# Pairing heads for larger weight loads, and untying slot copies from the next load, in a linear-attention and expert kernel

## The chip, the cores and the metric

The kernel runs on one core of one Trainium2 chip. The metric is the device time of one execution in microseconds (us); lower is better. A core has five engines with a queue each: TensorE (PE; weight loads are listed as PEld), VectorE (DVE), ScalarE (ACT), GpSimd (POOL) and SyncE (SP), and 16 DMA engines that all queues share. An engine works through its own instructions in the order in which the program gives them, and waits on semaphores for the others.

## The reference

Eight sequences, each of 576 positions, 8 heads of 64. Attention without a score matrix, then one expert of eight for each whole sequence:

```python
q_s = softmax(q, over head_dim);  k_s = softmax(k, over seq)
kv  = einsum('bhsd,bhse->bhde', k_s, v)
x   = einsum('bhsd,bhde->bhse', q_s, kv)        # -> [B, S, D = 512]
logits = x.mean(axis=1) @ w_gate                # [B, 8]
e_idx  = argmax(logits)                         # one expert for each sequence
out[b] = gate_w[b] * relu(x[b] @ w1[e]) @ w2[e] # w1 512x1024, w2 1024x512
```

The inputs are float32 and fixed; on them the eight sequences choose the experts 2 3 3 1 3 3 4 6. So 0, 1, 3, 6 and 7 need an expert whose weights were not there before, and 2, 4 and 5 use expert 3 again.

## The kernel before, in words

A sequence `b` is handled as two halves, `n = 2b` and `n = 2b + 1`, of four heads each; a half has four 64-row groups, kept as two "pairs" of heads side by side on 128 partitions.

- `load(n)` fetches q, k and v of a half on SyncE's queue: three transfers of 128 partitions x 1152 floats. Three buffers of each exist.
- `exp_q`, `exp_k` (ScalarE), `cast_v` (GpSimd) and `scale_q` (a sum and a reciprocal on VectorE, a multiply on GpSimd) prepare a half. `kvt_step` makes kv and transposes q on TensorE ("a kv step" here), with `kv_out` and `t_out` on VectorE. `x_step(n, g)` makes one quarter of x in the one `x` bank of PSUM, which VectorE empties with a running sum for the mean.
- `gate_step(b)` is the gate: four small matmuls, a chain of tiny VectorE operations for the argmax and for the look in `hist`, the history of which expert each of the five weight slots holds. GpSimd then reads the expert into a register and issues the loads of w1 (L314) and w2 (L325) into slot `b % 5`; when the expert is already in some slot, the loads are skipped at run time but still issued. These transfers convert float32 to float16 on the way. `gate_exp`, `gate_split` and `gate_spread` make the softmax weight.
- `fetch` (L367) copies w1 or w2, in two parts each, from the slot found at run time to the sequence's own slot; a sequence with fresh weights copies its slot onto itself. Since the source is a run-time index, the framework lets the copy wait for every weight load issued ahead of it.
- `moe(b)` is the expert: eight groups of `x @ w1` (L381, L386; Relu on ScalarE L390), then four outputs of `h @ w2` (L400, scaled on ScalarE L407) and a tail (L415, L420). Outputs leave on SyncE's queue.

The order of the work is written by hand. `moe(b)` yields 17 times (8 groups, twice in each of 4 outputs, once after the tail), so "unit" 17 b + m is the place after yield m of sequence b, and `at(t, f)` puts a piece of the attention of later sequences at a unit. All five engines keep the order in which these pieces are written. Pieces at the same unit keep the order of the `at` calls: those of the loop over sequences come ahead of the fetches.

Of the kernel before, what the change touches and what calls it, by code (L numbers as in the profile page):

```python
# [10 lines left out]
FP16 = mybir.dt.float16  # L11
# [8 lines left out]
def kernel(  # L20
# [15 lines left out]
    nc = tc.nc  # L36
# [8 lines left out]
    ND = D // 128  # L45
    NS = 5
    IN_RANGE = "max_index over a row of 8 gives 0 to 7, and the columns past the slots never hold the maximum"

    consts = ctx.enter_context(tc.tile_pool(name="consts", bufs=1))
# [29 lines left out]
    nc.vector.memset(ones_row, 1.0)  # L79
    hist = consts.tile([1, 8], FP32)  # L80
    nc.vector.memset(hist, -1.0)
    own = consts.tile([1, NS, 8], FP32)
    nc.vector.memset(own, 0.0)
    for n in range(NS):
# [9 lines left out]
    w1_all = consts.tile([128, NS, ND, F], FP16, name="w1_all")  # L94
    w2_all = consts.tile([128, NS, NF, D], FP16, name="w2_all")

    wg_sb = consts.tile([128, ND, E], FP32)
    wg_src = moe_w_gate.rearrange("(i h g e) n -> i h e g n", i=2, h=2, g=2)

    def load_wg():  # L100
        for i in range(2):
            for h in range(2):
                nc.scalar.dma_start(
                    out=wg_sb[64 * h:64 * h + 64, 2 * i:2 * i + 2, :], in_=wg_src[i, h]
                )

    def pair_src(t, b, i):

        return t[b].rearrange("(i n g) (p j) d -> i (g p) n (j d)", i=2, n=2, p=64)[i]

    out_p = out.rearrange("b (p j) d -> b p j d", j=J)

    ins, halves, seqs = {}, {}, {}

    def load(n, names="qkv"):
        if n >= 2 * B:
            return
        b, i = divmod(n, 2)
        for name in names:
            x = in_pool.tile([128, 2, J * Dh], FP32, name=f"{name}_in")  # L120
            nc.sync.dma_start(out=x, in_=pair_src({"q": q, "k": k, "v": v}[name], b, i))
            ins[n, name] = x.rearrange("p n (j d) -> p n j d", j=J)
# [140 lines left out]
    def gate_step(b):  # L263
        pooled = seqs[b]["pooled"] if b else seqs["pooled"]
        pg = bank("x") if b else seqs["qb"][0][:, 32:64]
        for c in range(ND):
            nc.tensor.matmul(
                pg[0:1, 0:E], lhsT=pooled[:, c:c + 1], rhs=wg_sb[:, c, :],
                start=(c == 0), stop=(c == ND - 1),
            )  # L270
        zz = gat_pool.tile([1, E], FP32, name="zz")
        nc.vector.tensor_single_scalar(out=zz, in_=pg[0:1, 0:E], scalar=1.0 / S, op=ALU.mult)
        mx8 = gat_pool.tile([1, 8], FP32, name="mx8")
        nc.vector.max(out=mx8, in_=zz)
        eidx = gat_pool.tile([1, 8], U32, name="eidx")
        nc.vector.max_index(out=eidx, in_max=mx8, in_values=zz)
        slot = b % NS
        sidx = None
        if b:
            same = gat_pool.tile([1, 8], FP32, name="same")  # L280
            nc.vector.tensor_tensor(
                out=same, in0=hist, in1=eidx[0:1, 0:1].to_broadcast([1, 8]), op=ALU.is_equal
            )
            score = gat_pool.tile([1, 8], FP32, name="score")
            nc.vector.scalar_tensor_tensor(
                out=score, in0=same, scalar=2.0, in1=own[:, slot], op0=ALU.mult, op1=ALU.max
            )
            top = gat_pool.tile([1, 8], FP32, name="top")
            nc.vector.max(out=top, in_=score)
            fresh = gat_pool.tile([1, 1], U32, name="fresh")  # L290
            nc.vector.tensor_single_scalar(out=fresh, in_=top[:, 0:1], scalar=1.0, op=ALU.is_equal)
            sidx = gat_pool.tile([1, 8], U32, name="sidx")
            nc.vector.max_index(out=sidx, in_max=top, in_values=score)
        nc.vector.tensor_copy(out=hist[:, slot:slot + 1], in_=eidx[0:1, 0:1])
        nmx = gat_pool.tile([1, 1], FP32, name="nmx")
        nc.vector.tensor_single_scalar(out=nmx, in_=mx8[:, 0:1], scalar=-1.0, op=ALU.mult)
        e_val = nc.values_load(
            eidx[0:1, 0:1], engines=[ET.Pool], min_val=0, max_val=E - 1,
            skip_runtime_bounds_check_because=IN_RANGE,
        )  # L300
        kw = {}
        if b:
            f_val = nc.values_load(  # L303
                fresh, engines=[ET.Pool], min_val=0, max_val=1,
                skip_runtime_bounds_check_because="is_equal gives 0 or 1",
            )
            kw = dict(cond=(f_val == 1))
        w1_src = moe_w1[ds(e_val, 1)].rearrange("o (i h g e) f -> i h e (o g) f", i=2, h=2, g=2)
        nh = 1 if b else 2
        for fh in range(nh):  # L310
            fs = slice(fh * F // nh, (fh + 1) * F // nh)
            for i in range(2):
                for h in range(2):
                    nc.gpsimd.dma_start(  # L314
                        out=w1_all[64 * h:64 * h + 64, slot, 2 * i:2 * i + 2, fs], in_=w1_src[i, h][:, :, fs], **kw
                    )
        seqs[b].update(zz=zz, nmx=nmx, sidx=sidx, e_val=e_val, kw=kw)
        if b:
            load_w2(b)

    def load_w2(b):
        w2_src = moe_w2[ds(seqs[b]["e_val"], 1)].rearrange("o (c p) n -> p (o c) n", p=128)
        for hf in range(2):
            cs = slice(4 * hf, 4 * hf + 4)
            nc.gpsimd.dma_start(out=w2_all[:, b % NS, cs], in_=w2_src[:, cs], **seqs[b]["kw"])  # L325

    def warm(count):

        pw = bank("ht")
        for n in range(count):  # L330
            nc.tensor.matmul(pw[:, 0:128], lhsT=ident, rhs=blkmask, start=True, stop=True)

    def gate_exp(b):
        ex = gat_pool.tile([1, E], FP32, name="ex")
# [23 lines left out]
    def fetch(b, w_all, part):  # L358

        if "src" not in seqs[b]:  # L360
            seqs[b]["src"] = nc.values_load(
                seqs[b]["sidx"][0:1, 0:1], engines=[ET.DVE], min_val=0, max_val=NS - 1,
                skip_runtime_bounds_check_because=IN_RANGE,
            )
        half = w_all.shape[2] // 2
        cs = slice(part * half, (part + 1) * half)
        nc.vector.tensor_copy(  # L367
            out=w_all[:, b % NS, cs],
            in_=w_all[:, ds(seqs[b]["src"], 1), cs].rearrange("p o c f -> p (o c) f"),
        )  # L370

    def moe(b):
        xt = seqs[b]["xt"]
# [57 lines left out]
    NU = 17  # L431
    ticks = {}

    def at(t, fn, *args):
        ticks.setdefault(t, []).append((fn, args))

    def at_gate(t, b):
        at(t, gate_step, b)
        at(t + 1, gate_exp, b)
        at(t + 2, gate_split, b)  # L440
        at(t + 4, gate_spread, b)
# [3 lines left out]
    at(3.5, gate_spread, 0)  # L445
    at_gate(2, 1)
    for b in range(2, B):
        u = 24 if b == 2 else 34 + 15 * (b - 3)
        for i in range(2):
            n, t = 2 * b + i, u + 4 * i  # L450
            at(t, kvt_step, n)
            for g in range(2):
                at(t + 2 + g, x_step, n, g)
            at(t - 4.2, exp_q, n)
            at(t - 4.2, cast_v, n)
            at(t - 3.2, exp_k, n)
            if n + 3 < 2 * B:
                at(t - 3.2, load, n + 3)
            at(t - 2.8, scale_q, n, nc.gpsimd)
        at_gate(u + 8, b)  # L460
    for b in range(1, B):
        for part in range(2):
            at(NU * b - 2 + part, fetch, b, w1_all, part)
            at(NU * b + 0.5 + part, fetch, b, w2_all, part)
    times = sorted(ticks)
    done = [0]

# [13 lines left out]
    with tc.manual_schedule(engines={ET.PE, ET.DVE, ET.Activation, ET.Pool, ET.SP}):  # L481

        warm(55)
        exp_q(0)
        scale_q(0, nc.vector)
        exp_k(0)
        exp_q(1)
        cast_v(0)
        scale_q(1, nc.gpsimd)
        load(3)  # L490
        t_step(0)
        q_sum_step(0)
        kv_step(0)
        exp_k(1)
        cast_v(1, True)
        x_step(0, 0)
        t_step(1)
        q_sum_step(1)
        kv_step(1)
        x_step(0, 1)  # L500
        pool_step()
        cast_v(2)
        gate_step(0)
        exp_q(2)
        x_step(1, 0)
        exp_k(2)
        x_step(1, 1)
        scale_q(2, nc.vector)
        exp_q(3)
        kv_step(2)  # L510
        exp_k(3)
        scale_q(3, nc.vector)
        cast_v(3, True)
        t_step(2)
        gate_exp(0)
        kv_step(3)
        x_step(2, 0)
        gate_split(0)
        t_step(3)
        x_step(2, 1)  # L520
        load_w2(0)
        for b in range(B):
            for m, _ in enumerate(moe(b)):
                run_ticks(NU * b + m + 1)
            if b == 0:
                for n in (4, 5, 6):
                    load(n)


# [28 lines left out]
```

## Time and profile before

| | |
|---|---|
| time, median of 3 runs | 256.33 us (255.81 to 257.01) |
| profiled execution, its time | 256.26 us |
| its span, first to last instruction | 254.6 us |
| TensorE busy, mean granted clock | 184.9 us, 0.868 |
| VectorE, ScalarE, GpSimd busy | 112.3, 113.7, 68.1 us |
| moved by DMA | 48.55 MB in 28790 packets |

In the profile's lines, `out<-in` are tiles by the program's names, `xN` is a count, and in a timeline the first two numbers are the start and the length in us; brackets hold the idle time of the engine before the line and what ended it. A line of waits reads: engine and line, what it waited for, us in total, times, longest. The granted clock is 1.00 at full speed. `w_all` stands for both weight tiles.

### The profile page before, as it was taken

The numbers are of one execution on the slowest core, as the hardware profiler recorded it, in microseconds if no ns is written. First come the engines' busy times: TensorE is split into PE (matmuls) and PEld (weight loads), VectorE is DVE, ScalarE is ACT, GpSimd is POOL, SyncE is SP. The second block draws the span as 40 slices with busy tenths as digits, with TensorE's granted clock in tenths as the row PEclk, the third lists the DMA queues.
The fourth block names the chain that finished last, engine by engine and source line by source line (L and its number), as shares of the span: only waits on it lengthen the run. The fifth ranks groups of instructions, "written<-read, shape, count | busy, mean of one in ns | idle before, by whom it ended". The sixth has DMA issues, their size and how long they took to land. (4 is left out here: it accounts for less than half of the span.)

```text
span 254.6 us, 4684 instructions
## 1 busy us (share of the span) xinstructions
PE 184.9 (73%) x1703; PEld 98.3 (39%) x1703; DVE 112.3 (44%) x357; ACT 113.7 (45%) x177; POOL 68.1 (27%) x88
## 2 busy tenths in 40 slices
PE   7465899939863699467398499869958820499991
PEld 7342454514431354224144254434534410145541
DVE  1759450223784765170644955576526600610000
ACT  3759654529343337513057127722842410034641
POOL 1327314005623122921006300630573060000000
PEclk9755699997996899989689979997999985589998
DMA  6997989999999912999607940850499389006134
GB/s 220 390 391 176 143 135 177 242 372 392 391 393 300 344 46 50 203 290 296 236 0 205 370 170 3 261 182 24 67 169 214 71 126 197 7 0 160 28 82 103
DMA packets 28790, 48.55 MB, mean 191 GB/s; under 512 B 3168, under 2 KB 10336, under 8 KB 28768
## 3 DMA queue, kind: packets, MB, share of 16 engines
q1 hardware_dynamic: 19456, 37.76, 44.0%
q0 software_dynamic: 8736, 10.49, 25.6%
q8 instruction: 13, 0.21, 0.3%
q10 hardware_dynamic: 576, 0.02, 0.1%
q14 instruction: 9, 0.07, 0.1%
HBM read 61.88 MB, written 9.44 MB: 280 GB/s over the span
## 5 line engine op out<-in xcount | busy, mean ns | idle before, releaser
L381 PE MATMUL mm<-xt,w_all 128*128 128x512 f16 x256 | 75.6, 426 | 17.7 <-DVE w_all L367 13.1
L390 ACT ACTIVATE hsb<-mm 128x512 f16<-128x512 f32 x64 | 37.8, 597 | 75.5 <-PE mm L381 75.3
L400 PE MATMUL mm<-w_all,hsb 128*128 128x512 f16 x256 | 59.4, 379 | 0.0
L381 PEld LDWEIGHTS <-w_all 128*128 128x128 f16 x256 | 22.2, 106 | 58.2 <-issue 28.5
L367 DVE COPY w_all<-w_all 128x2048 f16 x28 | 20.8, 748 | 41.3 <-DMA w_all<-in_moe_w_dram 25.1
L407 ACT ACTIVATE osb<-mm,gate 128x512 f32<-128x512 f32 x32 | 22.0, 686 | 33.8 <-PE mm L400 27.6
L314 POOL DMA_DIRECT2D w_all<-in_moe_w_dram x36 | 15.2, 427 | 76.2 <-DMA w_all<-in_moe_w_dram 34.1
L147 POOL TENSOR_TENSOR eq<-eq,qsi 128x1152 f16<-128x1152 f16 x13 | 27.8, 2139 | 27.1 <-DVE qsi L146 21.9
L400 PEld LDWEIGHTS <-hsb 128*128 128x128 f16 x256 | 23.2, 98 | 25.8
L134 POOL CAST va<-v_in 128x1152 f16<-128x1152 f32 x14 | 16.7, 1192 | 32.4 <-DMA v_in<-in_v_dram 32.2
L386 PEld LDWEIGHTS <-w_all 128*128 128x128 f16 x256 | 17.7, 105 | 18.2 <-issue 5.6
L232 DVE CUSTOM_DVE_ANT_0 xt<-x,ones_f 128x576 f16<-128x576 f32 x26 | 19.4, 744 | 12.2 <-PE x L222 12.2
L221 PE MATMUL x<-qt,kv 128*128 128x512 f16 x32 | 14.8, 462 | 13.7 <-DVE qt L191 5.5
L144 DVE TENSOR_REDUCE qs<-eq 128x18 f32<-128x1152 f16 x16 | 21.5, 1345 | 6.4 <-ACT eq L126 6.4
L126 ACT ACTIVATE eq<-q_in 128x1152 f16<-128x1152 f32 x16 | 18.6, 1160 | 6.2 <-DMA q_in<-in_q_dram 6.2
L386 PE MATMUL ht<-xt,w_all 128*128 128x64 f16 x256 | 19.2, 201 | 0.0
L138 ACT ACTIVATE ek<-k_in 128x1152 f16<-128x1152 f32 x16 | 18.6, 1162 | 0.8 <-DMA k_in<-in_k_dram 0.8
L170 DVE RECIPROCAL icv<-kv 128x1 f32<-128x1 f32 x30 | 4.9, 162 | 30.3 <-PE kv L183 29.0
L162 PE MATMUL kv<-va,ek 64*128 64x129 f16 x270 | 13.1, 248 | 6.3 <-POOL va L134 4.4
L162 PEld LDWEIGHTS <-ek 64*128 64x128 f16 x288 | 11.3, 110 | 11.3 <-issue 9.1
L183 PE MATMUL kv<-ident,eq 64*128 64x64 f16 x270 | 7.8, 203 | 8.5 <-POOL eq L147 5.2
L352 PE MATMUL x<-hl,ones_row 1*128 1x2 f16 x8 | 1.4, 171 | 14.7 <-DVE hl L344 14.7
(79 smaller groups left out, 146.7 us busy)
## 6 DMA issues: line engine op xcount, KB each, us to landing
q_in<-in_q_dram SPq DMA_DIRECT2D x16, 576.0 KB, 7.7
k_in<-in_k_dram SPq DMA_DIRECT2D x16, 576.0 KB, 8.4
v_in<-in_v_dram SPq DMA_DIRECT2D x16, 576.0 KB, 8.8
w_all<-in_moe_w_dram POOLq DMA_DIRECT2D x16, 512.0 KB
out_dram<-osb SPq DMA_DIRECT2D x64, 128.0 KB, 5.7
w_all<-in_moe_w_dram POOLq DMA_DIRECT2D x28, 256.0 KB
w_all<-in_moe_w_dram POOLq DMA_DIRECT2D x8, 128.0 KB
out_dram<-osb_t SPq DMA_DIRECT2D x16, 64.0 KB, 4.1
```

What stands on the lines that cost most here:

```text
L126: nc.scalar.activation(out=eq.rearrange("p j n d -> p n j d"), in_=ins.pop((n, "q")), func=AF.Exp)
L138: nc.scalar.activation(out=ek.rearrange("p j n d -> p n j d"), in_=ins.pop((n, "k")), func=AF.Exp)
L144: nc.vector.tensor_reduce(out=qs, in_=eq, op=ALU.add, axis=AX.X)
L147: eng.tensor_tensor(out=eq, in0=eq, in1=qsi.unsqueeze(3).to_broadcast([128, J, 2, Dh]), op=ALU.mult,)
L162: nc.tensor.matmul(kps[g][:, 0:129], lhsT=ek[r, j], rhs=va[r, j], start=(j == 0), stop=(j == J - 1),)
L232: nc.vector.tensor_tensor_reduce(out=xt[:, c, :], in0=px[:, 0:S], in1=ones_f32.to_broadcast([128, S]), scale=1.0, scalar=0.0, op0=ALU.mult ...
L367: nc.vector.tensor_copy(out=w_all[:, b % NS, cs], in_=w_all[:, ds(seqs[b]["src"], 1), cs].rearrange("p o c f -> p (o c) f"),)
L381: nc.tensor.matmul(phm, lhsT=w1_sb[:, c, fsl], rhs=xt[:, c, 0:SM], start=(c == 0), stop=(c == ND - 1),)
L386: nc.tensor.matmul(pht[:, fc * ST:(fc + 1) * ST], lhsT=w1_sb[:, c, fsl], rhs=xt[:, c, SM:S], start=(fc == 0 and c == 0), stop=(fc == NF - ...
L390: nc.scalar.activation(out=hsb[:, fc, 0:SM], in_=phm, func=AF.Relu)
L400: nc.tensor.matmul(po, lhsT=hsb[:, fc, st * 128:st * 128 + 128], rhs=w2_sb[:, fc, :], start=(fc == 0), stop=(fc == NF - 1),)
L407: nc.scalar.mul(osb, po, gate)
```

## The change

1. The heads of a half are paired otherwise: half `i` now holds heads 2i, 2i+1 and 4+2i, 4+2i+1, in place of 4i to 4i+3. A 64-row half of the partitions then needs one block of w1's rows, and w1 comes in 2 DMAs for 4 (4 for 8 in sequence 0); with the 2 of w2 a sequence's weights are 4 DMAs. The gate's weights come in 2 for 4.
2. At gate `b` the entry of slot `(b + 2) % 5` is taken out of the history, and a slot copy of `b` is declared independent of the loads of `b + 1` that were issued ahead of it. With the draw above the same sequences load and skip.
3. Half 4 (the first of sequence 2) is loaded ahead of sequence 0's expert, but SyncE first waits for a tiny copy out of w1 of sequence 0. Halves 5 and 6 follow at unit 14, in place of all three after sequence 0.
4. The units move. Sequence 2's kv steps stand at 20 and 28 (24 and 28 before), sequence 3's at 33 and 38 (34 and 38), later ones 14 units apart and 5 within a sequence (15 and 4); x steps follow by 2 and 4 units (2 and 3). Preparation comes 1.2 units earlier, the multiply of `scale_q` 1.4. The gates of 2 to 7 stand at 33, 43, 57, 71, 85, 99 (32, 42, 57, 72, 87, 102). Fetches of w1 stand at 17 b - 0.8 and - 0.6 (17 b - 2 and - 1), of w2 at 17 b + 1 and + 2 (+ 0.5 and + 1.5).

```diff
+    held = consts.tile([1, 8], FP16)
...
-    wg_src = moe_w_gate.rearrange("(i h g e) n -> i h e g n", i=2, h=2, g=2)
+    wg_src = moe_w_gate.rearrange("(h c e) n -> h e c n", h=2, c=ND)
...
-        return t[b].rearrange("(i n g) (p j) d -> i (g p) n (j d)", i=2, n=2, p=64)[i]
+        return t[b].rearrange("(n i g) (p j) d -> i (g p) n (j d)", i=2, n=2, p=64)[i]
...
         nc.vector.tensor_copy(out=hist[:, slot:slot + 1], in_=eidx[0:1, 0:1])
+        gone = (b + 2) % NS
+        nc.vector.memset(hist[:, gone:gone + 1], -1.0)
...
-            for i in range(2):
-                for h in range(2):
-                    nc.gpsimd.dma_start(
-                        out=w1_all[64 * h:64 * h + 64, slot, 2 * i:2 * i + 2, fs], in_=w1_src[i, h][:, :, fs], **kw
-                    )
+            for h in range(2):
+                issued[b].append(nc.gpsimd.dma_start(
+                    out=w1_all[64 * h:64 * h + 64, slot, :, fs], in_=w1_src[h][:, :, fs], **kw
+                ))
...
+    def hold_loads():
+        nc.sync.dma_start(out=held, in_=w1_all[64:65, 0, ND - 1, 0:8])
...
-        nc.vector.tensor_copy(
+        copy = nc.vector.tensor_copy(
             out=w_all[:, b % NS, cs],
             in_=w_all[:, ds(seqs[b]["src"], 1), cs].rearrange("p o c f -> p (o c) f"),
         )
+        for load_inst in issued.get(b + 1, ()):
+            tc.declare_no_dep(copy.ins, load_inst.ins, reason="...")
...
-        u = 24 if b == 2 else 34 + 15 * (b - 3)
+        u = 20 if b == 2 else 33 + 14 * (b - 3)
         for i in range(2):
-            n, t = 2 * b + i, u + 4 * i
+            n, t = 2 * b + i, u + i * (8 if b == 2 else 5)
             at(t, kvt_step, n)
             for g in range(2):
-                at(t + 2 + g, x_step, n, g)
-            at(t - 4.2, exp_q, n)
-            at(t - 4.2, cast_v, n)
-            at(t - 3.2, exp_k, n)
+                at(t + 2 + 2 * g, x_step, n, g)
+            at(t - 5.4, exp_q, n)
+            at(t - 5.4, cast_v, n)
+            at(t - 4.4, exp_k, n)
             if n + 3 < 2 * B:
-                at(t - 3.2, load, n + 3)
-            at(t - 2.8, scale_q, n, nc.gpsimd)
-        at_gate(u + 8, b)
+                at(t - 4.4, load, n + 3)
+            at(t - 4.2, scale_q, n, nc.gpsimd)
+        at_gate(t + 5, b)
     for b in range(1, B):
         for part in range(2):
-            at(NU * b - 2 + part, fetch, b, w1_all, part)
-            at(NU * b + 0.5 + part, fetch, b, w2_all, part)
+            at(NU * b - 0.8 + 0.2 * part, fetch, b, w1_all, part)
+            at(NU * b + 1 + part, fetch, b, w2_all, part)
+    at(14, load, 5)
+    at(14, load, 6)
...
         load_w2(0)
+        hold_loads()
+        load(4)
         for b in range(B):
             for m, _ in enumerate(moe(b)):
                 run_ticks(NU * b + m + 1)
-            if b == 0:
-                for n in (4, 5, 6):
-                    load(n)
```

More of the change, by code (lines that the diff above doesn't have):

```diff
@@ L97 @@
     wg_sb = consts.tile([128, ND, E], FP32)
-    wg_src = moe_w_gate.rearrange("(i h g e) n -> i h e g n", i=2, h=2, g=2)
+    wg_src = moe_w_gate.rearrange("(h c e) n -> h e c n", h=2, c=ND)
     def load_wg():
-        for i in range(2):
-            for h in range(2):
-                nc.scalar.dma_start(
-                    out=wg_sb[64 * h:64 * h + 64, 2 * i:2 * i + 2, :], in_=wg_src[i, h]
-                )
+        for h in range(2):
+            nc.scalar.dma_start(out=wg_sb[64 * h:64 * h + 64], in_=wg_src[h])
     def pair_src(t, b, i):
-        return t[b].rearrange("(i n g) (p j) d -> i (g p) n (j d)", i=2, n=2, p=64)[i]
+        return t[b].rearrange("(n i g) (p j) d -> i (g p) n (j d)", i=2, n=2, p=64)[i]
     out_p = out.rearrange("b (p j) d -> b p j d", j=J)
-    ins, halves, seqs = {}, {}, {}
+    ins, halves, seqs, issued = {}, {}, {}, {}
     def load(n, names="qkv"):
@@ L307, in gate_step @@
             kw = dict(cond=(f_val == 1))
-        w1_src = moe_w1[ds(e_val, 1)].rearrange("o (i h g e) f -> i h e (o g) f", i=2, h=2, g=2)
+        w1_src = moe_w1[ds(e_val, 1)].rearrange("o (h c e) f -> h e (o c) f", h=2, c=ND)
         nh = 1 if b else 2
+        issued[b] = []
         for fh in range(nh):
             fs = slice(fh * F // nh, (fh + 1) * F // nh)
-            for i in range(2):
-                for h in range(2):
-                    nc.gpsimd.dma_start(
-                        out=w1_all[64 * h:64 * h + 64, slot, 2 * i:2 * i + 2, fs], in_=w1_src[i, h][:, :, fs], **kw
-                    )
+            for h in range(2):
+                issued[b].append(nc.gpsimd.dma_start(
+                    out=w1_all[64 * h:64 * h + 64, slot, :, fs], in_=w1_src[h][:, :, fs], **kw
+                ))
         seqs[b].update(zz=zz, nmx=nmx, sidx=sidx, e_val=e_val, kw=kw)
@@ L324, in load_w2 @@
             cs = slice(4 * hf, 4 * hf + 4)
-            nc.gpsimd.dma_start(out=w2_all[:, b % NS, cs], in_=w2_src[:, cs], **seqs[b]["kw"])
+            issued[b].append(
+                nc.gpsimd.dma_start(out=w2_all[:, b % NS, cs], in_=w2_src[:, cs], **seqs[b]["kw"])
+            )
     def warm(count):
@@ L370, in fetch @@
         )
+        for load_inst in issued.get(b + 1, ()):
+            tc.declare_no_dep(
+                copy.ins, load_inst.ins,
+                reason="the slot that b + 1 loads into is taken out of the history before b looks for its source",
+            )
     def moe(b):
```

## The prediction, made before the change was timed

> **What bounds the kernel now.** I read the page's busy shares and DMA queues, then the chain that ended last, the waits, the TensorE timeline, and last the busy time between the moments at which each sequence's expert matmuls begin (found in that timeline).
>
> ```profile
> span 254.6 us, 4684 instructions
> PE 184.9 (73%) x1703; PEld 98.3 (39%) x1703; DVE 112.3 (44%) x357; ACT 113.7 (45%) x177; POOL 68.1 (27%) x88
> q1 hardware_dynamic: 19456, 37.76, 44.0%
> q0 software_dynamic: 8736, 10.49, 25.6%
> ```
>
> TensorE is busy 73%, and the two large queues fill the 16 DMA engines for 69.6% of the span, 177 us. No engine is full, so it is waits that count. The chain's middle, then the waits that matter:
>
> ```profile
> 206.59 8.23 DMA w_all<-in_moe_w_dram
> 214.82 3.12 issue
> 217.94 0.70 DVE w_all L367
> ...
> 219.64 0.21 DVE hl L344
> ...
> 219.89 0.16 PE x L352
> ```
>
> ```profile
> PE x L352 <- DVE hl L344: 14.7, 1, 14.7
> PE mm L381 <- DVE w_all L367: 13.1, 6, 6.1
> PE x L221 <- DVE qt L191: 5.5, 1, 5.5
> PE mm L381 <- ACT hsb L390: 4.2, 1, 4.2
> PE x L221 <- DVE pooled L232: 4.5, 5, 1.1
> ```
>
> In the chain the slot copy of sequence 6 (L367) starts only when sequence 7's weights have landed; behind it in VectorE's queue stands sequence 7's gate split (L344), for which TensorE waits 14.7 us in the middle of sequence 6. Six other waits, 13.1 us, are the first matmul of a sequence waiting for its copies. 5.5 us is TensorE waiting for VectorE while that waits for sequence 3's w2; 4.2 us is ScalarE's exp of sequence 2 standing ahead of a Relu until its q has landed. The last row is the x bank: up to 1.1 us when two quarters of x follow too closely.
>
> Stages: start of sequence 0's matmuls to 1's, and so on, the last to the end.
>
> ```profile
> 29.44:47.15 17.71, 17.71 (x129) 8.95 (x127) 5.35 (x25) 9.88 (x19) 3.90 (x6) 0.97 1.01 172
> 47.15:80.33 33.18, 21.55 (x202) 10.89 (x200) 15.93 (x42) 16.39 (x24) 10.02 (x11) 0.92 1.06 363
> 80.33:111.06 30.73, 23.17 (x238) 12.52 (x239) 16.53 (x57) 13.87 (x21) 12.26 (x12) 0.92 0.68 182
> 111.06:145.05 33.99, 24.43 (x206) 11.97 (x206) 17.67 (x50) 12.62 (x20) 8.84 (x11) 0.85 0.73 222
> 145.05:172.33 27.28, 22.58 (x237) 12.05 (x237) 16.33 (x54) 12.68 (x20) 6.77 (x10) 0.94 0.50 164
> 172.33:198.79 26.46, 22.35 (x206) 11.22 (x206) 14.86 (x48) 12.53 (x20) 10.41 (x10) 0.94 0.60 115
> 198.79:233.34 34.55, 19.07 (x122) 9.02 (x122) 7.47 (x26) 8.36 (x16) 3.95 (x6) 0.75 0.51 92
> 233.34:254.57 21.23, 15.91 (x114) 7.90 (x112) 0.00 (x0) 8.97 (x15) 0.00 (x0) 0.95 0.34 80
> ```
>
> The first two columns are length and TensorE's busy time, the last three granted clock, DMA share, GB/s. A bare sequence is 15.9 us of matmuls. Busy time holds slow matmuls too:
>
> ```profile
> 116.56 0.70 PE L162 MATMUL kv<-va,ek 64*128 64x129 f16 x18
> 117.46 1.04 PE L381 MATMUL mm<-xt,w_all 128*128 128x512 f16 x4
> ...
> 204.00 1.03 PE L381 MATMUL mm<-xt,w_all 128*128 128x512 f16 x4
> 219.98 1.89 PE L381 MATMUL mm<-xt,w_all 128*128 128x512 f16 x4
> ```
>
> Four matmuls take 1.03 us, and 1.89 after the long wait. Some two groups run so after each wait of about 1.7 us or more: I charge 1.7 us. A kv step costs 117.46 - 116.56 = 0.9.
>
> **The change, part by part.** Units are the yields, 17 per sequence.
>
> *Slot copies freed.* Gate 7 stands at 99 now, ahead of both fetches of 6 (101.2 to 104); gate 6 at 85, ahead of the w2 fetch of 5 (86, 87). With the ordering gone these copies need only their own load. Load 6 has a whole stage to land and load 7 more, so the 14.7 us go, and 1.7 of slow matmuls behind them. The history costs one more tiny memset per gate, in VectorE idle time.
>
> *Four weight DMAs for six.* Same bytes, same 4 KB rows, issued from GpSimd. Its value lies at gates on the path:
>
> ```profile
> 72.89 0.34 PE L267 MATMUL x<-wg_sb,pooled 128*1 128x8 f32 x8
> 78.08 0.05 POOL L314 DMA_DIRECT2D w_all<-in_moe_w_dram  x1 [1.39 <-DMA w_all<-in_moe_w_dram]
> 79.58 1.42 DVE L367 COPY w_all<-w_all 128x2048 f16 x2 [2.07 <-DMA w_all<-in_moe_w_dram]
> 96.88 0.27 PE L267 MATMUL x<-wg_sb,pooled 128*1 128x8 f32 x5
> 99.77 2.77 POOL L314 DMA_DIRECT2D w_all<-in_moe_w_dram  x4 [9.22 <-DVE hl L343]
> 102.73 1.52 POOL L325 DMA_DIRECT2D w_all<-in_moe_w_dram  x2 [0.18 <-DVE qs L144]
> 110.31 1.42 DVE L367 COPY w_all<-w_all 128x2048 f16 x2 [0.56 <-DMA w_all<-in_moe_w_dram]
> 122.21 0.69 DVE L367 COPY w_all<-w_all 128x2048 f16 x1 [8.23 <-DMA w_all<-in_moe_w_dram]
> 200.78 0.34 PE L267 MATMUL x<-wg_sb,pooled 128*1 128x8 f32 x8
> ```
>
> Skipped loads (gate 2) cost 1.5 us from the first of four issues to the copy; two cost 0.75. Issued w1 pieces take 2.77/4 = 0.69 each with 128 rows; one of twice the rows costs between 0.69 and 1.38, and I take 0.75, because a w2 piece of 512 rows takes 1.52/2 = 0.76. So each gate gains 0.75 us skipped and 1.2 issued; where the gate is off the path this is worth nothing, as matmuls cover it. At the start, two gate-weight DMAs fewer on ScalarE's queue: between 0 and 1.3 us, I take 0, since inputs are still arriving.
>
> *Third sequence's loads early.* Sequence 2's first half (1152 floats on 128 partitions, three times: 1.77 MB) is issued once w1 of sequence 0 lands, before 29.44, where it was issued behind sequence 0's outputs. At the 363 GB/s of stage 1 it takes 4.9 us of DMA time from the weights of 0 and 1; some is free:
>
> ```profile
> 36.00:38.00 2.00, 2.00 (x21) 1.05 (x18) 0.49 (x3) 1.20 (x2) 1.20 (x2) 1.00 0.14 21
> 44.53 0.69 ACT L407 ACTIVATE osb<-mm,gate 128x512 f32<-128x512 f32 x1 [1.04 <-PE mm L400]
> L126 ACT ACTIVATE eq<-q_in 128x1152 f16<-128x1152 f32 x16 | 18.6, 1160 | 6.2 <-DMA q_in<-in_q_dram 6.2
> L144 DVE TENSOR_REDUCE qs<-eq 128x18 f32<-128x1152 f16 x16 | 21.5, 1345 | 6.4 <-ACT eq L126 6.4
> 142.69 2.30 DVE L367 COPY w_all<-w_all 128x2048 f16 x1
> ```
>
> SyncE holds nothing else while it waits; the outputs come later. But the exp of half 4 now stands in stage 0 (14.6), and its q sums (15.8) just ahead of the fetch of sequence 1. ScalarE is free of its third output at 45.2; exp to 46.4, reduce to 47.7, reciprocal 48.0; two copies at the chain's 0.70 end at 49.4. That delays sequence 1 from 47.15 to 49.5. Its weights were there at 47.15; pushed back by 4.9 less the 1.7 left free at 36 to 38 they come by 50.4 at worst. The 4.2 us in stage 1 go.
>
> A GpSimd multiply beside a copy stretches it: 2.30 us at 142.69 against 0.70. The Trainium skill, "SBUF — State Buffer", section "Who interferes with whom", says that a copy in a two-port mode and GpSimd take one pair of ports in turns for whole instructions; the trace agrees (2.30). By that rule, freed copies that fall beside GpSimd's descriptor writing would pay 1.6 each, and the sum would be some 5 us longer.
>
> **The stages anew** (full-speed work, then waits).
> - 0: 17.7 + 2.4 (above) = 20.1.
> - 1: work 21.0 (21.55 less 1.7 slow, one kv step and quarter steps more); slow 1.7; behind w2 of 1, which the loads of half 5 now meet, between 0 and their 4.9, I take 1.5, as VectorE needs it only after six groups; 0.5 for the x bank. Gate 2 now ends the stage. Its load could be issued 99.77 - 96.88 = 2.9 after the gate's matmul, as at gate 3; with 0.75 for the skipped pieces and a copy 4.4, against 79.58 - 72.89 + 0.7 = 7.4 before. A kv step (0.9) and the gate itself (0.3) fill part: wait 3.2. 27.9.
> - 2: gate 3 to copies was 110.31 - 96.88 = 13.4; less 1.2 issue, plus a copy, 12.9. Up to the gate 11.7 of work (9.6 of the bare sequence, a kv step 0.9, x steps and gate 1.2), 1.7 slow, 0.8 bank. 27.1.
> - 3: work 20.9 (24.43 less two slow phases), slow 1.7. w2 of 3 was copied 25.3 after its gate (122.21 - 96.88). One of the two input loads that shared that window now comes ahead of the gate; between 20.4 (4.9 less) and 25.3 I take 22.5. That is 22.5 - 12.9 = 9.6 into the stage; with a copy and an x step VectorE is free at 11.1, and TensorE needs it at 8.8 (slow 1.7, six groups, a kv step): wait 2.3, slow 1, bank 1, copies of 4 behind a kv step 1.5. 28.4.
> - 4: 22.58 less 1.7 slow and one kv step: 20.0; slow 1.7, bank 0.8, copies behind an x step 1.5. 24.0.
> - 5: 22.35 less slow and an x step: 20.5; slow 1.7, bank 0.8; GpSimd now casts half 14 before it issues load 6. 23.0.
> - 6: bare 15.9, gate pieces and an x step 0.3, copies 0.3. 16.5.
> - 7 and end: 21.2.
>
> Sum 188.2; with 29.4 ahead, span 217.6. The profiled execution lies 1.7 above its span (256.26 against 254.6, the median at 256.33): 219.3, say **219**.
>
> **The rivals.**
> *A. The ordering stays, in fact.* The copies of 5 and 6 then wait for loads 6 and 7, since both gates come first now. Gate 7 to copy was 217.94 - 200.78 = 17.2 us. Sequence 5 loses that less 4 us of matmuls, plus 1.7; sequence 6's start the 13.4 of a w1 less 2.8. 219 + 15 + 11 = 245. For it: the copy reads a slot picked at run time, so every load could be its source. Against: load 7's slot is named out of bounds by the diff.
> *B. The early stages keep their waits.* If w2 of 3 still takes 25.3 and sequence 2 starts at 80.33 as now (3.2 later), plus 3 for slow matmuls: 219 + 2.8 + 3.2 + 3 = 228. For it: DMA share 1.01 and 1.06 in stages 0 and 1.
> *C. Freed copies collide with descriptor writing:* four by 1.6, 225 at most.
> *D. Slower: the new w1 pieces move at less than half speed,* if a 1 MB piece of 64 partitions spreads worse. w1 took 110.31 - 99.77 = 10.5. A factor f adds 10.5(f-1) at the starts of 1 and 3, and the same less 8.6 and 6.6 of slack at 6 and 7 (gates 1.0 and 19.5 into stage 5, 13.4 to the copies, stages of 23.0 and 16.5): at f = 2.25 these make 13.1 + 13.1 + 4.5 + 6.5 = 37, no gain; at 2.5, 16 + 16 + 7 + 9 = 48, 267. Against: pieces of 64 partitions and 4 KB rows are what is moved already. The Trainium skill, "DMA: Bandwidth & Descriptors", section "Rules for kernel authors", says that halves of the partitions share the same 16 engines either way; by that rule the factor is 1. No trace here shows the new piece.
>
> **How the numbers follow.** Forecast 0.68 (209 to 226 alone), C 0.10, B 0.13, A 0.05, D 0.03, otherwise no change 0.01. The low end, 207: stage 0's 2.4, the 1.5 in each of 1, 3 and 4, and 2.3 with two slow phases all absent (12). The high end takes in B with a lock or two: 233. The runs shown spread by 0.47%, so under 0.5% tells nothing. Faster 0.96, within 0.01, slower 0.03.
>
> **What would show it.** TensorE's wait for L344 gone; no copy of 5 or 6 waiting for the next load; sequence 1's start near 49.5, 2's near 77, 3's near 104; stage 6 near 16.5; four POOL DMAs per gate. It is wrong if a copy still waits 10 us or more late in the run, if a w1 takes well over 10.5 us, or if the early weights come later than the exp of half 4 hides.

## The result, and the profile after

The changed kernel takes 227.49 us (median of 4 runs, 225.91 to 228.89) against 256.07 (255.18 to 257.01) for the kernel before: a ratio of 0.888, with an interval of 0.881 to 0.895, or 28.6 us less. Ratios, here and below, leave out disturbed runs, so that they can differ a little from the quotient of two medians, while the traces of three kernels (sums earlier, the sum of half 4 behind the copies, all w2 copies later) are of such a run. The forecast was 219, with 207 to 233 as its range: right in direction and within the range, but 8.5 us too low. It lies above 226, the high end that the forecast's own mechanism had; only the room left for rival B holds it. The profiled execution is the longest of the four, 228.89 us with a span of 227.2.

The head of the page after:

```profile
span 227.2 us, 4594 instructions
PE 181.5 (80%) x1703; PEld 96.1 (42%) x1703; DVE 118.0 (52%) x365; ACT 112.9 (50%) x177; POOL 60.6 (27%) x70
```

TensorE's busy time fell by 3.4 us only; what went is waiting. VectorE has more busy time than before (118.0 against 112.3) though its work is the same but for eight tiny memsets, so some of its instructions got longer. The waits after:

```profile
PE mm L393 <- DVE w_all L374: 18.4, 6, 6.3
PE x L359 <- DVE hl L351: 5.2, 4, 2.1
PE x L219 <- DVE pooled L230: 4.3, 4, 3.5
```

The single wait of 14.7 us for the gate's split is gone (that row, now L351, holds four waits of at most 2.1). What is left is the first matmul of a sequence waiting for its slot copies, 18.4 us in six waits. Stages as before, from one sequence's first expert matmul to the next's, five of the eight rows (the columns as in the prediction), and all of them in a table:

```profile
29.42:52.11 22.69, 18.92 (x129) 9.21 (x127) 7.71 (x28) 12.32 (x22) 6.01 (x6) 0.93 1.13 244
...
78.07:111.38 33.31, 24.46 (x205) 11.92 (x205) 19.12 (x56) 13.01 (x22) 12.50 (x10) 0.81 0.72 200
...
140.97:165.19 24.22, 20.38 (x206) 10.61 (x206) 17.09 (x51) 13.84 (x22) 6.67 (x8) 1.00 0.47 140
165.19:188.13 22.94, 20.14 (x209) 10.51 (x210) 17.38 (x63) 11.07 (x21) 9.69 (x9) 1.00 0.74 144
188.13:206.07 17.94, 17.82 (x114) 8.43 (x114) 5.15 (x9) 8.02 (x13) 1.64 (x3) 0.90 0.91 167
...
```

| stage | before | forecast | after | after less forecast |
|---|---|---|---|---|
| 0 | 17.7 | 20.1 | 22.7 | +2.6 |
| 1 | 33.2 | 27.9 | 26.0 | -1.9 |
| 2 | 30.7 | 27.1 | 33.3 | **+6.2** |
| 3 | 34.0 | 28.4 | 29.6 | +1.2 |
| 4 | 27.3 | 24.0 | 24.2 | +0.2 |
| 5 | 26.5 | 23.0 | 22.9 | -0.1 |
| 6 | 34.6 | 16.5 | 17.9 | +1.4 |
| 7 and end | 21.2 | 21.2 | 21.1 | -0.1 |

Stage 6 alone gives 16.6 of the 27.4 us that the span lost. Stages 0 and 2 are longer than before. Where stages 0 to 3 went wrong is read in the timeline, all engines, only the lines that matter (gates are the `wg_sb` matmuls):

```profile
47.56 1.35 DVE L142 TENSOR_REDUCE qs<-eq 128x18 f32<-128x1152 f16 x1 [7.98 <-ACT eq L124]
...
48.95 0.27 DVE L144 RECIPROCAL qsi<-qs 128x18 f32<-128x18 f32 x1
...
49.39 2.11 POOL L145 TENSOR_TENSOR eq<-eq,qsi 128x1152 f16<-128x1152 f16 x1 [7.02 <-ACT ek L136]
49.97 2.81 DVE L374 COPY w_all<-w_all 128x2048 f16 x2 [0.76 <-DMA w_all<-in_moe_w_dram]
...
73.27 0.35 PE L265 MATMUL x<-wg_sb,pooled 128*1 128x8 f32 x8
76.12 0.05 POOL L315 DMA_DIRECT2D w_all<-in_moe_w_dram  x1 [1.47 <-DMA w_all<-in_moe_w_dram]
...
77.32 1.42 DVE L374 COPY w_all<-w_all 128x2048 f16 x2 [0.17 <-issue]
...
93.31 0.35 PE L265 MATMUL x<-wg_sb,pooled 128*1 128x8 f32 x8
93.43 1.35 DVE L142 TENSOR_REDUCE qs<-eq 128x18 f32<-128x1152 f16 x1 [0.18 <-ACT eq L124]
...
95.33 2.12 POOL L145 TENSOR_TENSOR eq<-eq,qsi 128x1152 f16<-128x1152 f16 x1 [11.57 <-DVE zz L270]
...
95.93 1.52 DVE L279 TENSOR_TENSOR same<-hist,eidx 1x8 f32<-1x8 f32 x1
...
99.18 1.36 POOL L315 DMA_DIRECT2D w_all<-in_moe_w_dram  x2 [1.74 <-DVE hl L350]
...
110.63 1.42 DVE L374 COPY w_all<-w_all 128x2048 f16 x2 [5.88 <-DMA w_all<-in_moe_w_dram]
111.38 1.89 PE L393 MATMUL mm<-xt,w_all 128*128 128x512 f16 x4 [6.26 <-DVE w_all L374]
121.84 1.42 DVE L374 COPY w_all<-w_all 128x2048 f16 x2 [3.88 <-DMA w_all<-in_moe_w_dram]
123.99 0.38 PE L219 MATMUL x<-qt,kv 128*128 128x512 f16 x1 [3.54 <-DVE pooled L230]
```

The reader is to see two places. Around 50, GpSimd's multiply starts 0.6 us ahead of sequence 1's two copies, which then take 2.81 us instead of 1.42. After gate 3 at 93.31, a q sum (L142) stands first in VectorE's queue; the reciprocal behind it releases GpSimd's multiply (by the program, which reads the reciprocal there; the brackets name a neighbour), and beside that the gate's compare of eight numbers (L279) takes 1.52 us. The weights of sequence 3 are first asked for 99.18 - 93.31 = 5.87 us after the gate.

### The profile page after: what moved, and what is told of

Its sections match the earlier page's. It is cut to its first block, busy times and chain, and to the rows that moved or that the text cites. A ratio compares the mean times of both kernels' runs of the same rounds, so it can differ in the third digit from the quotient of the medians.

```text
span 227.2 us, 4594 instructions
## 1 busy us (share of the span) xinstructions
PE 181.5 (80%) x1703; PEld 96.1 (42%) x1703; DVE 118.0 (52%) x365; ACT 112.9 (50%) x177; POOL 60.6 (27%) x70
## 3 DMA queue, kind: packets, MB, share of 16 engines
q0 software_dynamic: 8544, 10.49, 28.5%
## 4 chain that ended last, share of the span: by engine, by line
PE 43%; DVE 22%; DMA 20%; ACT 5%; issue 5%; POOL 1%; DVEq 1%; POOLq 0%; ACTq 0%
DMA w_all<-in_moe_w_dram 16%; PE mm L393 16%; PE mm L412 15%; DVE qs L142 5%; DVE w_all L374 4%; PE kv L160 3%; DVE same L279 2%; PE x L219 2%; ACT eq L124 2%; PE ht L398 2%; DMA k_in<-in_k_dram 2%; DVE kv L170 2%; DMA q_in<-in_q_dram 2%; PE mm L427 2%; DVE xt L230 2%
## 5 line engine op out<-in xcount | busy, mean ns | idle before, releaser
L393 PE MATMUL mm<-xt,w_all 128*128 128x512 f16 x256 | 74.3, 421 | 18.9 <-DVE w_all L374 18.4
L402 ACT ACTIVATE hsb<-mm 128x512 f16<-128x512 f32 x64 | 37.6, 593 | 56.8 <-PE mm L393 56.7
L412 PE MATMUL mm<-w_all,hsb 128*128 128x512 f16 x256 | 60.9, 385 | 0.1
L393 PEld LDWEIGHTS <-w_all 128*128 128x128 f16 x256 | 21.7, 104 | 43.0 <-DVE w_all L374 23.5
L419 ACT ACTIVATE osb<-mm,gate 128x512 f32<-128x512 f32 x32 | 21.9, 684 | 29.3 <-PE mm L412 25.3
L374 DVE COPY w_all<-w_all 128x2048 f16 x28 | 21.1, 754 | 22.4 <-DMA w_all<-in_moe_w_dram 21.3
L142 DVE TENSOR_REDUCE qs<-eq 128x18 f32<-128x1152 f16 x16 | 21.5, 1346 | 13.9 <-ACT eq L124 13.9
L398 PEld LDWEIGHTS <-w_all 128*128 128x128 f16 x256 | 17.7, 104 | 18.2 <-issue 5.6
L132 POOL CAST va<-v_in 128x1152 f16<-128x1152 f32 x14 | 16.3, 1162 | 21.9 <-DMA v_in<-in_v_dram 21.7
L315 POOL DMA_DIRECT2D w_all<-in_moe_w_dram x18 | 8.3, 463 | 31.0 <-DVE hl L350 24.1
L160 PEld LDWEIGHTS <-ek 64*128 64x128 f16 x288 | 10.4, 105 | 11.8 <-issue 8.0
L160 PE MATMUL kv<-va,ek 64*128 64x129 f16 x270 | 12.1, 236 | 2.7 <-ACT qt L187 2.3
L170 DVE SCALAR_TENSOR_TENSOR kv<-kv,icv,blkmask 128x128 f16<-128x128 f32 x30 | 10.5, 351 | 1.1
L189 DVE COPY qt<-kv 128x576 f16<-128x576 f16 x24 | 10.7, 448 | 0.0
```

The source lines that it names most:

```text
L142: nc.vector.tensor_reduce(out=qs, in_=eq, op=ALU.add, axis=AX.X)
L160: nc.tensor.matmul(kps[g][:, 0:129], lhsT=ek[r, j], rhs=va[r, j], start=(j == 0), stop=(j == J - 1),)
L374: copy = nc.vector.tensor_copy(out=w_all[:, b % NS, cs], in_=w_all[:, ds(seqs[b]["src"], 1), cs].rearrange("p o c f -> p (o c) f"),)
L393: nc.tensor.matmul(phm, lhsT=w1_sb[:, c, fsl], rhs=xt[:, c, 0:SM], start=(c == 0), stop=(c == ND - 1),)
L398: nc.tensor.matmul(pht[:, fc * ST:(fc + 1) * ST], lhsT=w1_sb[:, c, fsl], rhs=xt[:, c, SM:S], start=(fc == 0 and c == 0), stop=(fc == NF - ...
L402: nc.scalar.activation(out=hsb[:, fc, 0:SM], in_=phm, func=AF.Relu)
```

## The experiments

### Which part brought it

**Freed copies taken back** from the changed kernel; the history still loses a slot at each gate:

```diff
-        for load_inst in issued.get(b + 1, ()):
-            tc.declare_no_dep(copy.ins, load_inst.ins, reason="...")
```

> The changed kernel with the slot copies ordered behind the next load again, all else kept. Theory (the freed copies carry the largest part, and the new places of the gates need them): the w2 copy of 5 waits for load 6 and the w1 copy of 6 for load 7, 15 and 11 us as worked out in rival A; 245 to 255 us, with TensorE idle for over 10 us in stage 5 and at the start of stage 6. Rival (the moved units alone carry the gain, the copies would be hidden): within 2 us of the changed kernel's 227.5.

Measured 254.39 us, ratio 0.994 (0.989 to 0.998). Its timeline late in the run:

```profile
185.58 0.69 DVE L374 COPY w_all<-w_all 128x2048 f16 x1 [14.39 <-DMA w_all<-in_moe_w_dram]
186.80 0.16 PE L359 MATMUL x<-hl,ones_row 1*128 1x2 f16 x1 [15.30 <-DVE hl L351]
...
212.89 1.46 PE L388 MATMUL mm<-xt,w_all 128*128 128x512 f16 x3 [10.19 <-DVE w_all L374]
```

The copy of sequence 5 waits 14.39 us for a later load, the gate's split behind it in VectorE's queue holds TensorE for 15.30, and sequence 6 starts 10.19 late. That is rival A's mechanism in its two places, at 25.5 us where it was priced at 26. In the new order the freed copies are worth 254.4 - 227.5 = 27 us.

**Freed copies alone**, put into the kernel before:

```diff
+        gone = (b + 2) % NS
+        nc.vector.memset(hist[:, gone:gone + 1], -1.0)
...
+        for load_inst in issued.get(b + 1, ()):
+            tc.declare_no_dep(copy.ins, load_inst.ins, reason="...")
```

> The kernel before with the history entry taken out and the copies freed, nothing else. Theory: only the 14.7 us wait in stage 6 and its 1.7 us of slow matmuls go: 256.1 - 16.4 = 239.7, range 237 to 243, stages 0 to 5 unchanged. Rival (the wait is replaced by another on load 6 or on the outputs): above 246.

Measured 239.89, ratio 0.936 (0.929 to 0.942): 16.3 us, as expected. Its row for stage 6:

```profile
200.24:217.58 17.34, 16.61 (x121) 8.26 (x122) 6.09 (x25) 8.36 (x16) 3.95 (x6) 1.00 0.79 137
```

17.34 instead of 34.55: the wait and the half-speed matmuls behind it are gone.

**Pairing alone**, put into the kernel before (with it the lines on the heads and on the gate's weights, as in the change):

```diff
-        w1_src = moe_w1[ds(e_val, 1)].rearrange("o (i h g e) f -> i h e (o g) f", i=2, h=2, g=2)
+        w1_src = moe_w1[ds(e_val, 1)].rearrange("o (h c e) f -> h e (o c) f", h=2, c=ND)
...
-            for i in range(2):
-                for h in range(2):
+            for h in range(2):
```

> The kernel before with the heads paired and w1 and the gate's weights in half as many DMAs, nothing else. Theory: 0.75 us less at gate 2 and about 1.2 us at gate 3, and up to 1.2 at load 7: 253 to 255.5. Rival D (a piece of 64 partitions and 1 MB moves more slowly): over 258, with w1 of sequence 3 over 11.5 us from first issue to copy. Rival (issue time is all hidden): 256 within 0.7.

Measured 253.08, ratio 0.988 (0.982 to 0.994): 3.1 us. At its gate 3:

```profile
98.60 1.36 POOL L310 DMA_DIRECT2D w_all<-in_moe_w_dram  x2 [9.23 <-DVE hl L339]
108.86 1.42 DVE L363 COPY w_all<-w_all 128x2048 f16 x2 [1.73 <-DMA w_all<-in_moe_w_dram]
```

Two pieces of w1 are issued in 1.36 us and stand in the buffer 10.26 us after the first issue, against 10.54 for four pieces. The factor f of rival D is 1, and it falls. The gates gain little: from gate to the sequence's start 0.9 us at gate 2 (6.50 for 7.44) and 0.3 at gate 3 (13.90 for 14.18). Most of the gain lies in stage 5, 23.7 us for 26.5: TensorE waits about 1 us less for a GpSimd cast, which stands behind two issues fewer, and the granted clock was 1.00 for 0.94. With the freed copies alone stage 5 ran at 1.00 too, so that part need not be the pairing's.

**Pairing taken back** from the changed kernel (the same lines the other way):

> The changed kernel with the old pairing of heads and w1 in 4 DMAs (8 for sequence 0). Theory: the two more pieces cost 0.9 us of GpSimd at a skipped gate and 1.3 us at a loaded one; on the path at gates 2 and 3: 228.5 to 230.5. Rival (off the path or bandwidth-bound): 227.5 within 0.8.

Measured 231.03, ratio 0.900 (0.892 to 0.907; the changed kernel's interval, 0.881 to 0.895, still meets it): about 3.5 us. In its profiled execution gate 0 came at 20.88, against 18.72 in the changed kernel and 18.73 in the kernel before, which has the same pairing; so 2.2 us of that execution lie at a late first gate, which the pairing alone doesn't explain.

Together: the pairing is worth about 3 us or less, the freed copies 16 in the old order and 27 in the new one. The new order with the pairing but without the freed copies (254.4) is no faster than the pairing alone in the old order (253.1). So the order pays only with the freed copies, while these pay 16 without it; order and pairing then add 12.4 (239.9 to 227.5).

### The hold and the third sequence's loads

**No hold:** `hold_loads()` left out, so that half 4 is asked for at once.

> The changed kernel with half 4 loaded at once, without SyncE's wait for w1 of sequence 0. Theory: 1.77 MB at some 390 GB/s take 4.5 us ahead of or beside w1 of sequence 0, but TensorE comes to it only at 29.4: sequence 0 starts 0 to 2 us later, the w1 of 1 comes a little sooner; 227.5 within 1.5. Rival (the wait is what protects w1): sequence 0 starts 3 us or more later, 230 or more.

Measured 230.5, ratio 0.900 (0.891 to 0.909), 3 us above the changed kernel, but with intervals that overlap, so that the difference isn't clear of the spread. Sequence 0 starts 0.8 later (30.24), as the theory had it, while the time is the rival's. Stages 3 and 4 are 1.2 longer each and stage 2 is 1.2 shorter; what makes that stays open.

**Half 4 late:** no hold and no early load; half 4 comes by `at(14, load, 4)`, ahead of halves 5 and 6.

> The changed kernel without the wait on w1 and with half 4 loaded at unit 14 with 5 and 6. Theory: its q lands near 52, the exp at unit 14.6 holds ScalarE until then, sequence 1 starts near 56 instead of 52.1 while its weights come sooner: 2 to 5 us over 227.5. Rival (stage 1 is bound by the same input bytes either way): 227.5 within 1.

Measured 238.35, ratio 0.931 (0.922 to 0.941): 10.9 us slower where 2 to 5 were expected. Its timeline at the end of stage 0:

```profile
55.26 1.16 ACT L124 ACTIVATE eq<-q_in 128x1152 f16<-128x1152 f32 x1 [9.69 <-DMA q_in<-in_q_dram]
...
58.86 5.71 DVE L374 COPY w_all<-w_all 128x2048 f16 x4 [0.75 <-DVE qsi L144]
59.94 1.04 PE L393 MATMUL mm<-xt,w_all 128*128 128x512 f16 x2 [12.37 <-DVE w_all L374]
```

The exp waits 9.69 us for its q, the sum behind it blocks VectorE, and all four copies of sequence 1 stand behind that: TensorE waits 12.37. So in the new order the early load is a condition, not a gain by itself: this order puts sequence 1's copies behind half 4's sum.

### Why the changed kernel lies 8.5 us above the forecast

My theory was that VectorE's queue is to blame at two places: the q sum ahead of gate 3, and the sum ahead of sequence 1's copies. The rival: crowded DMA engines make the weights of 3 late in any case.

**Sum of each first half three units earlier**, so that it stands well ahead of the gate:

```diff
+            a = 3 if b > 2 and i == 0 else 0
-            at(t - 5.4, exp_q, n)
+            at(t - a - 5.4, exp_q, n)
...
+            at(t - a - 4.2, scale_q, n, nc.gpsimd)
```

> The changed kernel with exp, cast and sums of the first half of sequences 3 to 7 three units earlier, loads where they were. They stand just ahead of the gates 3 to 6 now. Theory (the q sum and the GpSimd multiply beside the compare hold up those gates, the failed term of stage 2): gate 3 to its first weight issue falls from 5.9 to about 2.9 us, stage 2 from 33.3 to about 30.5, and the waits of the gate spread at 3, 5 and 6 (2.2, 2.0, 0.8) go: 220 to 224. Rival (load 3 is bound by DMA bandwidth, not by its issue): 226 to 228.5, the copies of 3 no more than 0.5 us earlier after the gate.

Measured 227.46, ratio 0.886 (0.877 to 0.895): no gain, where 220 to 224 were expected. Yet the step itself did what it should:

```profile
94.23 0.35 PE L265 MATMUL x<-wg_sb,pooled 128*1 128x8 f32 x8
95.52 0.15 DVE L279 TENSOR_TENSOR same<-hist,eidx 1x8 f32<-1x8 f32 x1
97.67 1.37 POOL L315 DMA_DIRECT2D w_all<-in_moe_w_dram  x2 [3.09 <-DVE hl L351]
...
109.74 1.42 DVE L374 COPY w_all<-w_all 128x2048 f16 x2 [6.58 <-DMA w_all<-in_moe_w_dram]
...
120.72 1.42 DVE L374 COPY w_all<-w_all 128x2048 f16 x2 [2.81 <-DMA w_all<-in_moe_w_dram]
```

The compare is back at 0.15 and the first weight goes out 3.44 us after the gate instead of 5.87. This shows the cause of 2.4 of the late microseconds: 1.4 are the compare, the rest is the sum. The w1 copy still comes 12.1 after that issue, and the w2 copy, 23.0 after it, still blocks VectorE in stage 3 (TensorE waited 4.04 at 124.44 for an x step).

**The same with the input loads moved too** (`at(t - a - 4.4, load, n + 3)`), so that load 11 is asked for ahead of the gate:

> As the kernel with the sums three units earlier, and the input loads issued beside them three units earlier too, so that the load of half 11 is done before gate 3. Theory (these input loads share the DMA engines with load 3): w1 of 3 lands 1 to 3 us sooner after its first issue than 11.5 us, w2 of 3 sooner than 22.7 by 3 to 5: 2 to 5 us below the kernel with the sums alone. Rival (sharing costs nothing there): the same within 1 us.

Measured 226.7, ratio 0.887 (0.880 to 0.895).

```profile
95.82 1.36 POOL L315 DMA_DIRECT2D w_all<-in_moe_w_dram  x2 [3.23 <-DVE hl L351]
107.21 1.42 DVE L374 COPY w_all<-w_all 128x2048 f16 x2 [6.03 <-DMA w_all<-in_moe_w_dram]
118.44 1.42 DVE L374 COPY w_all<-w_all 128x2048 f16 x2 [3.60 <-DMA w_all<-in_moe_w_dram]
```

From issue to copy 11.39 for w1 and 22.62 for w2, against 11.45 and 22.66 in the changed kernel and 12.07 and 23.05 with the sums alone: where the input loads were issued made little difference. But the edit did not take them out of the weights' way. Between first issue and w2 copy SyncE's queue moved 3.51 MB here, 3.33 in the changed kernel and 3.74 in the kernel before, and the two large queues together took 103, 99.5 and 107% of the 16 engines' time (packets overlap, so this can pass 100; the weights alone 56.7, 56.4 and 57.3). So the weights shared full engines in all three. That this sharing sets the 22.6 fits, but it is not shown: no run had fewer input bytes in that stretch.

**Sum of half 4 behind the copies:** `at(16.6 if n == 4 else t - 4.2, scale_q, n, nc.gpsimd)`.

> The changed kernel with the q sum and the GpSimd multiply of half 4 moved from unit 15.8 to 16.6, behind the w1 copies of sequence 1. Theory (the multiply stretches the first of these copies, 2.1 us against 0.7, on the path): sequence 1 starts at 50.7 instead of 52.1 and the time falls by 1 to 1.5 us: 226 to 226.5. Rival (the landing of w1 of 1 sets the start, the stretch is hidden): 227.5 within 0.7, sequence 1 at 51.8 or later.

Measured 226.6 (223.48 to 228.83), ratio 0.876 (0.868 to 0.885), which overlaps the changed kernel's 0.881 to 0.895.

```profile
46.51 1.42 DVE L374 COPY w_all<-w_all 128x2048 f16 x2 [7.41 <-DMA w_all<-in_moe_w_dram]
...
56.38 1.42 DVE L374 COPY w_all<-w_all 128x2048 f16 x2 [6.88 <-DMA w_all<-in_moe_w_dram]
...
58.68 0.38 PE L219 MATMUL x<-qt,kv 128*128 128x512 f16 x1 [3.40 <-DVE qt L189]
```

Sequence 1 starts at 48.22 instead of 52.11, without a wait, and its weights had landed by 46.51: the sum and the multiply made the whole wait of 3.63 us that ended stage 0. But the w2 copy, reached sooner, now waits 6.88 us for its load with VectorE blocked, and TensorE loses 3.40 behind it. Stage 0 lost 3.7 us and stage 1 gained 3.4.

**All w2 copies five units later:** `at(NU * b + 6.2 + 0.2 * part, fetch, b, w2_all, part)`.

> The changed kernel with the w2 copies at units 6.2 and 6.4 of their sequence in place of 1 and 2. Theory (in stage 3 these copies wait in VectorE's queue for w2 of 3 and hold up the x quarters and gate 4 behind them, as the copies of 6 did before the change): the 3.5 us wait of x goes, and about 1 us of slow matmuls: stage 3 near 26, 222 to 224.5. Rival (w2 of 3 is late in any case, and the first output waits for it instead): 226.5 to 228.5, with a wait of 2 us or more ahead of the outputs of 3.

Measured 234.44, ratio 0.906 (0.897 to 0.916): slower. In stage 3:

```profile
122.37 1.35 DVE L142 TENSOR_REDUCE qs<-eq 128x18 f32<-128x1152 f16 x1
...
124.60 1.79 DVE L279 TENSOR_TENSOR same<-hist,eidx 1x8 f32<-1x8 f32 x1
...
127.15 1.40 DVE L374 COPY w_all<-w_all 128x2048 f16 x2
127.88 5.30 PE L412 MATMUL mm<-w_all,hsb 128*128 128x512 f16 x12 [3.88 <-DVE w_all L374]
```

The x wait is gone, but the copy now stands behind the next sum and a stretched compare, and TensorE waits for it 3.88 us and then runs slow (12 matmuls in 5.30). The load was not what it waited for: the copy's row shows no wait of its own. Stage 3 is 2.3 us longer than in the changed kernel, and stage 5, where the w2 copies take 3.03 beside a multiply and TensorE waits 3.01 for them, 4.7.

**The three edits together:**

> The changed kernel with three edits: w2 copies at 6.2 and 6.4, the preparation and loads of the first halves of 3 to 7 three units earlier, the sum of half 4 behind the copies of 1. Theory (the gain of the earlier sums, 2 us at gate 3, was given back because a sum then stood behind the blocked w2 copy; with the copy moved it stays): 217 to 221. Rival (each edit only moves a wait to the next load of 3): 222 or more.

Measured 222.31, ratio 0.868 (0.862 to 0.873), above the 217 to 221 of the theory and at the 222 that the rival began with.

```profile
84.94 3.03 DVE L374 COPY w_all<-w_all 128x2048 f16 x2
87.30 1.04 PE L412 MATMUL mm<-w_all,hsb 128*128 128x512 f16 x4 [3.01 <-DVE w_all L374]
...
165.65 3.03 DVE L374 COPY w_all<-w_all 128x2048 f16 x2
```

Two late copies, those of 2 and 5, now fall beside a GpSimd multiply: 3.03 instead of 1.42 us each time, and TensorE waits.

**w2 copies late only where the load is late**, otherwise as in the last kernel:

```diff
+            late = 5.2 - 0.8 * part if b in (1, 3, 6, 7) else 0
+            at(NU * b + 1 + part + late, fetch, b, w2_all, part)
```

> The three edits together, but with the w2 copies at 6.2 and 6.4 only in sequences 1, 3, 6 and 7, whose weights are fresh, and at 1 and 2 in 2, 4 and 5, whose copies wait for nothing. Theory (in the run of the three edits the late copies of 2 and 5 fell behind a q sum and beside a GpSimd multiply, and TensorE waited 3.0 us for them in each of stages 2 and 5): both waits and the slow matmuls after them go, 3 to 4.5 us each where on the path; stage 5 falls from 27.8 to about 23, stage 2 is partly given back to the landing of load 3: 215 to 219. Rival (run to run the stages trade waits, the copies' place is no cause): 221 to 223.5.

Measured 216.49 (215.48 to 217.72), ratio 0.843 (0.839 to 0.848): faster than both kernels. The group of the gates' compares, in the changed kernel and in this one (minimum, median, maximum in ns):

```profile
L279 DVE TENSOR_TENSOR same<-hist,eidx x7: 153/1524/1795, 35.5 to 185.0; 1x8 f32<-1x8 f32 x7
```

```profile
L279 DVE TENSOR_TENSOR same<-hist,eidx x7: 153/153/155, 34.3 to 172.8; 1x8 f32<-1x8 f32 x7
```

Not one compare is stretched any more. Its largest wait left is 8.26 us at the start of sequence 3, whose w1 copy comes 12.1 us after its first issue (90.98 to 103.08). Only the w2 copies of 2, 4 and 5 were moved since the last kernel, and that took 5.8 us. Against the changed kernel, the order of the preparation and of the copies took 11 us, more than the forecast had missed, with as many bytes to move and a w1 of 3 that came no sooner after its issue.

## Why the prediction was right, and where it was off

**Right.** The freed copies: both of rival A's waits appear when the ordering is put back and are gone without it; stage 6 came to 17.9 against 16.5 (TensorE was busy for 17.82 of it, at a granted 0.90). The pairing: 1.36/2 = 0.68 a piece (0.75 taken), no slower transfer. At gate 2 the copy begins 4.05 us after the gate's matmul, sequence 2 starting 4.8 after it (4.4 taken). Stages 4 and 5 came to within 0.2, but by two errors that cancel: TensorE was idle 3.8 us in stage 4 (24.22 - 20.38), where I had put 2.3 of waits and 1.7 of slow matmuls behind them, and the clock was 1.00. In stage 5 it was idle 2.8 against 0.8, at 1.00 again. That these two came out so close is luck. In stage 1 the 1.5 behind w2 of 1 was not paid.

**The step that failed: stage 2's "gate 3 to copies was 13.4; less 1.2 issue, plus a copy, 12.9".** From gate 3 to the first matmul it was 111.38 - 93.31 = 18.1, so 5.2 too little, and the gate itself came 1.0 later in its stage than taken. The term was carried over from the kernel before, whose gate had no sum ahead of it. Here the sum of half 8 is due at 42.8 (33 + 14 - 4.2) and gate 3 at 43 (33 + 5 + 5). I had done this reading for stage 0, and not for the gates. From gate to first issue it took 5.87 where 2.9 was carried over, 3.0 too little; 2.4 of these went when the sums were moved. From that issue to the copy I allowed 10.54 - 1.2 = 9.3, and it took 11.45, 2.1 too little: the 1.2 of saved issue shortened this to 10.26 only, as the pairing alone shows, so the end of the transfer sets it and not the last issue. What makes it another 1.2 longer in the new order no run shows; in that stretch SyncE's queue moved 1.58 MB, against 0.84 with the pairing alone.

**Stage 0's 2.4.** The sum's delay was seen and its follower missed: the multiply that the sum releases runs beside the two copies I priced at 0.70 each. The two took 2.81, and the first matmul came at 52.11, not 49.5. Of the 2.6 missed, 1.2 is this longer wait (3.63 us) and 1.2 is TensorE's busy time, 18.92 against 17.71 (this stage began with slow matmuls). A smaller term was left out as well: the copies start 0.75 after the reciprocal's end (49.22). Here the row puts this down to the load, but with half 4 late the same 0.75 is put down to the reciprocal, and the program reads the slot's number there. I had rival C on the table, a copy beside GpSimd, but only for freed copies and descriptor writing; it struck the start of sequence 1 and, in a form not on the list, the compare at the gates. The Trainium skill, "SBUF — State Buffer", section "Who interferes with whom", states that a VectorE instruction with two SBUF inputs also contends with a GpSimd instruction that reads SBUF. The runs agree: the compare reads two tiny SBUF tiles and takes 1.52 to 1.79 us beside the multiply, 0.15 away from it; at gate 3 the two end together, at 97.45.

**w2 of 3, 22.5 taken,** was copied 121.84 - 93.31 = 28.5 after its gate. Of these 6.0 the late issue is 3.0, and 2.8 is what I had taken off the old 25.3: from issue to copy it took 22.66, in the kernel before 22.44. My reason for the lower figure, an input load out of its way, fails: SyncE's queue moved 3.33 MB in that stretch against 3.74 before, not the 1.77 less that one load would make. Since sequence 3 started as much later, stage 3 paid only 1.2.

**Rival B named about this number, 228, with another mechanism.** Its sequence 2 at 80.33 did not come (78.07), and the 8.5 us did not need emptier DMA engines to go: with the sums and copies reordered, and as many bytes to move, the time is 216.5. The crowd itself is still there: the longest wait of that kernel, 8.26 us, is for a w1 that shares the engines with inputs and outputs.

## What to carry to other kernels

When work is moved, redo the queue around every gate and every copy: what stands ahead of it on the same engine, and what GpSimd starts when that is done. A delay read from the old order is not a term for the new one. An in-order engine that runs both helper work and copies that wait for DMA should meet each copy only when its load has landed: late where the load is fresh, early where it was skipped, since one late offset for all was slower here (222.3 against 216.5, two kernels alike in all else).

## What the runs showed of the hardware that was not expected

A compare of eight numbers in one partition can take 1.79 us (0.15 alone) because a GpSimd multiply of 128 x 1152 runs beside it; a pair of copies went from 1.42 to 2.81 and 3.03. Slow matmuls did not follow every wait: TensorE ran at a granted 1.00 through stages 4 and 5 though 1.63 and 1.47 us of waiting began them, and at 0.90 in stage 6 after 1.85.
